# Attention with routed experts on one core: rows of the last ten expert tiles turned by the DMA, and a second staging buffer for weights

## The chip, the core and the metric

The kernel runs on one core of a Trainium2 chip. The metric is device time in microseconds (us) of one launch. Engines are named as in the profile: PE is TensorE (PEld its weight loads), DVE is VectorE, ACT is ScalarE, POOL is GpSimd, SP is SyncE, which issues most DMAs.

## The reference, cut to what matters

```python
q_rot, k_rot = (rotate(q), rotate(k))             # B=4, H=8, S=576, D=64
attn = softmax(scale * q_rot @ k_rot.T)
x = (attn @ v).transpose(0, 2, 1, 3).reshape(B, S, 512)
logits = x @ w_gate                               # 8 experts
for b in range(B):
    for s in range(S):
        fresh_e = int(np.argmax(logits[b, s]))
        e = fresh_e if s == 0 or local_gate[b, s] < 0.5 else prev_e
        prev_e = e
        h = np.maximum(x[b, s] @ w1[e], 0.0)      # 512 -> 1024
        out[b, s] = p[e] * (h @ w2[e])            # 1024 -> 512
```

A token keeps its predecessor's expert unless its gate falls below one half, so tokens have to be sorted by expert before the expert products.

## The kernel before, in words

The first part of the program is attention over pairs of heads, then routing. The second part, which the change touches, works through tiles of 128 tokens, each tile of one expert. There are 19 of them, numbered 0 to 18. Tiles 0 to 5 (KE = 6 of them) are filled from the first three batches; tiles 6 to 18, the late tiles, are sorted when the routing of the last batch is known. LAST is 18. Code for further tiles stands behind a condition and isn't entered with these inputs.

With the reference's inputs the experts get 1152, 0, 0, 500, 0, 0, 606 and 46 tokens. The early tiles take experts 0, 0, 0, 0, 3, 3; the late tiles take 0 five times (tiles 6 to 10), 3 twice (11, 12), 6 five times (13 to 17) and 7 once (18). A late tile loads and splits weights only where its expert differs from that of the tile before (`need`), which is so in tiles 6, 11, 13 and 18.

All products are in fp32 as three passes over operands split into a high and a low part (`PASSES`). A tile t goes through these steps:

- `gather(t)`: POOL fetches 128 rows of x, with the token's probability behind them, by an indirect DMA.
- `turn_x(t)`: PE turns the 128x512 rows in four transposes into `tx`, ACT writes the high part `xs` (L303), DVE the low part (L307).
- `first_product(t)`: 24 matmuls give `h`, 128x1024 (L933). The first half goes through ACT's Relu (L943) and is turned by PE in `turn_h` (`th`, L967). The second half is turned by the DMA: DVE copies it into two planes of 16-bit halves (L942), SP stores them to `inner` in DRAM (L944), `land_h` reads them back by a DMA transpose (`ht`, L951), and `split_landed` makes high and low parts (ACT L957, DVE L958).
- `second_product(t)`: 24 matmuls give `o` (L976); ACT scales it by the probability (`os`, L981), POOL scatters the rows by an indirect DMA (L982).

Weights of one expert are eight pieces of 128x1024 (512 KB): k = 0 to 3 are the first matrix, 4 to 7 the second. `load_pair(t, c)` loads pieces 2c and 2c+1 into the one staging buffer `stage`, inside a condition on `need`. `split_w(t, c)` makes high parts (POOL L877 or ACT L875) and low parts (DVE or POOL L878) in the same kind of condition, and then issues `load_pair(t + 1, c)`.

The order of all this is written by hand, for late tiles in the string `TILE`. A letter is a step that is recorded on every engine's queue at that point, and each engine then runs its own queue in order: f is a quarter of the first product of tile t, s a quarter of the second product of tile t-1 (a last s records `os` and the scatter), x `turn_x(t+1)`, A and B the splits of the first matrix for t+1, C and D those of the second matrix for t, h `turn_h(t)`, T `land_h(t)`, H `split_landed(t-1)`, g a gather.

## Time and profile before

| what | value |
|---|---|
| measured, median of 3 (lowest to highest) | 549.04 us (548.77 to 549.04) |
| profiled execution, its own time | 548.69 us |
| its span in the trace | 546.8 us |
| PE busy | 520.2 us, 95% of the span |
| DVE, ACT, POOL busy | 401.7, 334.1, 327.6 us |
| mean granted clock of PE | 0.994 of full speed |

Times in the views are microseconds from the start of the span. The late tiles run from 372.43, where the first product of tile 6 starts, to 537, where the last product ends. The profiled execution's own time is 1.9 us more than its span.

### The profile page before, as it was taken

To read this page: it belongs to the slowest core of one execution; us is meant where nothing else is said; L and a number is where in the kernel's file an instruction comes from. 1 tells how busy PE (TensorE), PEld (TensorE's weight loads), DVE (VectorE), ACT (ScalarE), POOL (GpSimd) and SP (SyncE) were. 2 spreads that over 40 slices of the span, in tenths; PEclk is the share of its full clock that TensorE was granted. 3 is DMA by queue.
4 is the path that set the end of the run, shared out by engine and by line. 5 is a ranking of instruction groups with operands and counts; after the bars stand their busy time and mean duration, and the time that the engine had idled before them with its cause. 6 is when DMAs were issued, how large, how long until landed. Compare 5 with 4: busy or idle time off the path is not lost. (4 is left out here: it accounts for less than half of the span.)

```text
span 546.8 us, 10672 instructions
## 1 busy us (share of the span) xinstructions
PE 520.2 (95%) x3280; PEld 459.5 (84%) x3281; DVE 401.7 (73%) x736; ACT 334.1 (61%) x754; POOL 327.6 (60%) x243
## 2 busy tenths in 40 slices
PE   7989999999999999998999999999999998999992
PEld 4788999999999999997888788887888886888871
DVE  6898999999999999999999845348422757522650
ACT  2899889888998999987667523351421333422340
POOL 2997989888777988986698202355412453411341
PEclk9999999999999999999999999999999999999997
DMA  8759688776887787885288214553437394635350
GB/s 249 297 123 230 180 242 236 175 200 184 229 229 180 210 223 203 214 220 146 34 201 233 70 27 167 166 220 120 171 98 241 107 352 138 200 102 183 117 184 25
DMA packets 62024, 97.35 MB, mean 178 GB/s; under 512 B 27969, under 2 KB 38209, under 8 KB 59010
## 3 DMA queue, kind: packets, MB, share of 16 engines
q1 hardware_dynamic: 58914, 86.84, 55.4%
q0 software_dynamic: 3040, 9.71, 5.7%
q8 instruction: 28, 0.46, 0.3%
q14 instruction: 42, 0.34, 0.2%
HBM read 76.98 MB, written 12.86 MB: 164 GB/s over the span
## 5 line engine op out<-in xcount | busy, mean ns | idle before, releaser
L976 PE MATMUL o<-w,hs 128*128 128x512 f32 x456 | 113.5, 398 | 2.2 <-DVE hs L307 1.0
L272 DVE TENSOR_REDUCE mn<-s 128x1 f32<-128x576 f32 x144 | 107.3, 746 | 3.6 <-PE s L267 2.2
L933 PE MATMUL h<-w,xs 128*128 128x512 f32 x444 | 106.1, 392 | 0.9 <-DVE xs L307 0.6
L289 ACT ACTIVATE e<-s,mn 128x576 f32<-128x576 f32 x128 | 95.2, 744 | 18.7 <-DVE mn L272 15.4
L267 PE MATMUL s<-m,qst 128*128 128x288 f32 x512 | 97.4, 310 | 5.4 <-ACT e L289 3.2
L307 DVE TENSOR_TENSOR ptl<-tm,pth 128x512 fp32r<-128x512 f32 x139 | 95.1, 684 | 6.5 <-ACT pth L303 4.1
L976 PEld LDWEIGHTS o<-w,hs 128*128 128x128 f32 x456 | 83.0, 188 | 19.8 <-DVE hs L958 1.4
L982 POOL DMA_INDIRECT out_dram<-os,sidx x19 | 23.5, 1238 | 126.8 <-ACT os L981 79.7
L933 PEld LDWEIGHTS h<-w,xs 128*128 128x128 f32 x444 | 82.6, 188 | 19.1 <-DVE w L878 1.1
L303 ACT CAST pth<-tm 128x512 fp32r<-128x512 f32 x139 | 80.8, 582 | 12.3 <-PE tm L325 11.2
L267 PEld LDWEIGHTS s<-m,qst 128*128 128x128 f32 x512 | 74.7, 188 | 12.2 <-ACT e L289 6.2
L325 PE MATMUL tm<-wid,e 128*128 128x128 f32 x512 | 77.0, 272 | 1.3 <-ACT e L289 0.5
L361 PE MATMUL pv<-pth,v 128*128 128x288 f32 x256 | 76.4, 314 | 0.4 <-DVE ptl L307 0.2
L361 PE MATMUL pv<-ptl,v 128*128 128x288 f32 x256 | 76.5, 314 | 0.0
L196 POOL TENSOR_TENSOR stage<-stage 128x1152 f32<-128x1152 f32 x26 | 69.0, 2665 | 10.5 <-DMA stage<-in_qk_dram 10.5
L878 DVE TENSOR_TENSOR w<-stage,w 128x1024 fp32r<-128x1024 f32 x41 | 56.8, 1424 | 22.3 <-POOL w L877 13.9
L325 PEld LDWEIGHTS tm<-wid,e 128*128 128x128 f32 x512 | 62.0, 140 | 2.2 <-DVE ptl L307 1.0
L361 PEld LDWEIGHTS pv<-pth,v 128*128 128x128 f32 x256 | 48.2, 188 | 2.8 <-DVE ptl L307 0.9
L361 PEld LDWEIGHTS pv<-ptl,v 128*128 128x128 f32 x256 | 48.3, 189 | 0.0
L943 ACT ACTIVATE hr<-h 128x512 f32<-128x512 f32 x12 | 7.2, 599 | 50.5 <-DVE hr L942 50.5
L307 DVE TENSOR_TENSOR hs<-th,hs 128x512 fp32r<-128x512 f32 x26 | 17.4, 687 | 27.3 <-ACTq L884 17.0
L197 POOL TENSOR_TENSOR stage<-stage 128x576 f32<-128x576 f32 x26 | 36.9, 1430 | 0.2
(195 smaller groups left out, 815.4 us busy)
## 6 DMA issues: line engine op xcount, KB each, us to landing
stage<-in_wts_dram SPq DMA_DIRECT2D x70, 512.0 KB
stage<-in_qk_dram SPq DMA_DIRECT2D x13, 1152.0 KB
stage<-in_wts_dram SPq DMA_DIRECT2D x9, 1024.0 KB
qst<-xq SPq DMA_DIRECT2D x56, 128.0 KB
stage<-in_v_dram SPq DMA_DIRECT2D x16, 320.0 KB
m<-xq SPq DMA_DIRECT2D x14, 288.0 KB
m<-xk SPq DMA_DIRECT2D x14, 288.0 KB
m<-xq SPq DMA_DIRECT2D x14, 256.0 KB
```

The lines of the kernel that those rows point to most:

```text
L196: engine.tensor_tensor(x, x, tab[:, 2 * f:2 * f + 2], op=ALU.mult)
L197: engine.tensor_tensor(rr[:, f], x[:, 0], x[:, 1], op=ALU.add)
L267: pe.matmul(st[:, h, lo:hi], lhs, keys[:, k0:k0 + hi - lo], start=(n == 0), stop=(n == len(parts_) - 1))
L272: dve.tensor_reduce(mn, s_t[g][:, :, 0:HALF], axis=AX.XY, op=ALU.min)
L289: act.activation(dst.rearrange("p (h s) -> p h s", h=2), s_t.pop(g)[:, :, 0:HALF], AF.Exp, bias=mn, scale=-1.0, accum_out=sums[:, col:col ...
L303: act.copy(hi, src)
L307: dve.tensor_tensor(lo, src, hi.bitcast(F32), op=ALU.subtract)
L325: pe.transpose(ps[:, k], src[:, k * P:(k + 1) * P], ident)
L361: pe.matmul(pv_t[p, u], lhs.rearrange("p c d -> p (c d)"), rhs, start=(n == 0), stop=(n == 9))
L878: (pool if k in on_pool else dve).tensor_tensor(lo, src, hi.bitcast(F32), op=ALU.subtract)
L933: pe.matmul(ps[:, c], xs_t[t][:, x, k], w[y][:, c * 512:(c + 1) * 512], start=(k == 0 and n == 0), stop=(k == 3 and n == 2))
L976: pe.matmul(ps, hs_t[t][:, x, k], w[y][:, (k % 2) * 512:(k % 2 + 1) * 512], start=(k == 0 and n == 0), stop=(k == 7 and n == 2))
```

## The change

Ten tiles, 9 to 18, get their x rows turned in the way that the second half of `h` already goes (`X_DMA` is 9). Letter P: POOL copies the gathered rows of tile t+3 into two planes of 16-bit halves (`planes_x`) and keeps the probability aside (`keep_prob`). Letter T: behind the transpose of `ht`, SP issues the transpose `xt` for tile t+2 and the store of the planes of t+3 to `turned`. Letter x: ACT and DVE split `xt` of tile t+1, which is now read from SBUF and no longer from PSUM. Gathers come two tiles earlier; tile 6 issues three.

The two pieces of the 16-bit planes of `h` are copied by ACT where DVE did it. H stands before A now, and D behind the last s.

The first matrix of tile t+3 is loaded behind D, at L, of tile t; even tiles use a second staging buffer `other`, in space that early tiles had used. Each load has 512 KB; pairs of 1024 KB are gone. The loads of the second matrix stay at C and D.

```diff
@@ -47,8 +47,9 @@
 SPREAD_LAST = 127
 
 TILE_EARLY = ("ffAffsfxBssgCsshD", "ffAffxfsBsCsgsshD", "fffAffxBssChsgssD", "ffAfffxBsssshsCDg", "ffAfffBsssxsshCgD", "fffxAffsBssgssChD")
-TILE = "ffAgffHfxBTssshsCDs"
-TILE_LAST = "ffxAffHfssBsChsDss"
+TILE = "ffHAgPfffxBTssshsCsDL"
+X_DMA = KE + 3
+TILE_LAST = "ffHfffsssChsDss"
 PULL = 3
 PE_LAG = 2
 
@@ -169,6 +170,7 @@
 
     qtail = [const.tile([P, 2, P], F32R, name="qtail")] * 2
     rows_d = dram.tile([NT + 1, DX], F32, name="rows_d")
+    turned_d = [dram.tile([P, 2, 512], U16, name=f"turned_{i}") for i in range(2)]
     inner_d = [dram.tile([P, 2, 512], U16, name=f"inner_{i}") for i in range(2)]
 
     qkl = stage[:, 0:2304].rearrange("p (f s) -> p f s", f=4)
@@ -804,6 +806,7 @@
         return [plan, codes] + slots(lambda: st["codes"], NBLK, KE, NLATE) + [first_gather, experts_of]
 
     NTILE = KE + NLATE
+    LAST = KE + U_LATE - 1
     w_t, x_t, xs_t, h_t, hs_t = {}, {}, {}, {}, {}
     w_done = set()
     regs = {}
@@ -815,8 +818,15 @@
         )
 
     w_stage = []
-
-    def staged(k):
+    other = []
+
+    def staged(k, t=0):
+        if k < 4 and KE < t <= LAST and t % 2 == 0:
+            if not other:
+                two = over.tile([P, 2304], F32, tag="xq", name="other_0")
+                other.extend(two[:, i * 1024:(i + 1) * 1024] for i in range(2))
+                other.extend(over.tile([P, 1024], F32, tag=f"qst{i}", name=f"other_{2 + i}") for i in range(2))
+            return other[k]
         return stage[:, k * 1024:(k + 1) * 1024] if k < 7 else w_stage[0][:, 0:1024]
 
     def load_w(t, k):
@@ -833,9 +843,8 @@
         if t in regs:
             e, need = regs[t]
             with tc.If(need > 0):
-                for k, n in ((6, 1), (7, 1)) if c == 3 else ((2 * c, 2),):
-                    to = stage[:, k * 1024:(k + n) * 1024] if k < 7 else staged(7)
-                    sp.dma_start(to, wts[bass.ds(e, 1), :, k * 1024:(k + n) * 1024])
+                for k in (2 * c, 2 * c + 1):
+                    sp.dma_start(staged(k, t), wts[bass.ds(e, 1), :, k * 1024:(k + 1) * 1024])
 
     def split_early(k):
 
@@ -849,7 +858,7 @@
         w_t[0, k] = hi, lo
         w_done.add((0, k))
 
-    need_t, w_own, landed = {}, {}, {}
+    need_t, w_own, landed, prob_of, xs_src, planes_of = {}, {}, {}, {}, {}, {}
 
     def needs_of(t):
 
@@ -870,7 +879,7 @@
         def parts():
             for d in range(2):
                 k = 2 * c + d
-                src, hi, lo = staged(k), w[:, d, 0], w[:, d, 1]
+                src, hi, lo = staged(k, t), w[:, d, 0], w[:, d, 1]
                 if k in on_act:
                     act.copy(hi, src)
                 else:
@@ -891,7 +900,7 @@
             w_done.add((t, k))
             if t <= KE:
                 load_w(t + 1, k)
-        if t > KE:
+        if t > KE and c > 1:
             load_pair(t + 1, c)
 
     def gather(t):
@@ -939,18 +948,40 @@
             act.activation(h, ps.rearrange("p c n -> p (c n)"), AF.Relu)
             return
         planes = h[:, 512:].bitcast(U16).rearrange("p (l n) -> p l n", l=2)
-        dve.tensor_copy(planes, ps[:, 1].bitcast(U16).rearrange("p (n l) -> p l n", l=2))
+        act.copy(planes, ps[:, 1].bitcast(U16).rearrange("p (n l) -> p l n", l=2))
         act.activation(h[:, 0:512], ps[:, 0], AF.Relu)
         sp.dma_start(inner_d[t % 2], planes)
 
     def by_dma(t):
         return KE <= t < LAST
 
+    def turn_by_dma(name, src):
+        x = pk_p.tile([P, S], F32, tag="pk", name=name)[:, 0:512]
+        sp.dma_start_transpose(x.bitcast(U16).rearrange("p (k n) -> p k n", k=4), src.rearrange("t l n -> (t l) n"))
+        return x.rearrange("p (k n) -> p k n", k=4)
+
     def land_h(t):
-        x = pk_p.tile([P, S], F32, tag="pk", name=f"ht_{t}")[:, 0:512]
-        sp.dma_start_transpose(
-            x.bitcast(U16).rearrange("p (k n) -> p k n", k=4), inner_d[t % 2].rearrange("t l n -> (t l) n"))
-        landed[t] = x.rearrange("p (k n) -> p k n", k=4)
+        landed[t] = turn_by_dma(f"ht_{t}", inner_d[t % 2])
+
+    def keep_prob(t):
+        p = lg_all.rearrange("p j e -> p (j e)")[:, 100 + t - KE:101 + t - KE]
+        pool.tensor_copy(p, x_t[t][:, DM:DM + 1])
+        prob_of[t] = p
+
+    def planes_x(t):
+        x = pk_p.tile([P, S], F32, tag="pk", name=f"xp_{t}")[:, 0:512]
+        planes = x.bitcast(U16).rearrange("p (l n) -> p l n", l=2)
+        pool.tensor_copy(planes, x_t[t][:, 0:DM].bitcast(U16).rearrange("p (n l) -> p l n", l=2))
+        keep_prob(t)
+        planes_of[t] = planes
+
+    def split_x(t):
+        xs = v2_p.tile([P, 10, 2, D], F32R, tag="v2", name=f"xs_{t}")
+        xs = xs.rearrange("p j c d -> p (j c d)")[:, 0:1024].rearrange("p (l k n) -> p l k n", l=2, k=4)
+        x = xs_src.pop(t)
+        act.copy(xs[:, 0], x)
+        dve.tensor_tensor(xs[:, 1], x, xs[:, 0].bitcast(F32), op=ALU.subtract)
+        xs_t[t] = xs
 
     def split_landed(t):
         x, hs = landed.pop(t), hs_t[t]
@@ -978,7 +1009,7 @@
             if k % 2 == 1:
                 yield k
         o = et_p.tile([P, S], F32, tag="et", name=f"os_{t}")
-        act.activation(o[:, 0:DM], ps, AF.Copy, scale=x_t[t][:, DM:DM + 1])
+        act.activation(o[:, 0:DM], ps, AF.Copy, scale=prob_of[t] if t in prob_of else x_t[t][:, DM:DM + 1])
         done = pool.indirect_dma_start(
             out=outf, out_offset=bass.IndirectOffsetOnAxis(ap=sidx[:, t:t + 1], axis=0),
             in_=o[:, 0:DM], in_offset=None, bounds_check=NT - 1, oob_is_err=False)
@@ -986,7 +1017,8 @@
         tc.declare_no_dep(done.ins, group="rows out", reason="rows of their own")
         tc.add_to_no_dep_group("rows out", done.ins)
 
-    LAST = KE + U_LATE - 1
+    def ahead(t):
+        return [u for u in ((KE + 2, KE + 3) if t == KE else (KE + 1,) if t == KE - 1 else (t + 3,)) if KE < u <= LAST]
 
     def experts_phase():
         for t in range(LAST + 1):
@@ -1000,15 +1032,20 @@
                             finish()
                         if t < LAST:
                             needs_of(t + 1)
-                        if KE < t + 2 <= LAST:
-                            expert_of(t + 2)
+                        for u in ahead(t):
+                            expert_of(u)
                     if k is not None:
                         yield t
                 elif c == "s":
                     if next(second, None) is not None:
                         yield t
                 elif c == "x" and t < LAST:
-                    turn_x(t + 1)
+                    if t + 1 >= X_DMA:
+                        split_x(t + 1)
+                    else:
+                        turn_x(t + 1)
+                        if t + 1 >= KE:
+                            keep_prob(t + 1)
                 elif c in "AB" and t < LAST:
                     split_w(t + 1, "AB".index(c))
                 elif c in "CD" and t > 0:
@@ -1016,16 +1053,31 @@
                 elif c == "h":
                     turn_h(t)
                     yield t + 1
+                elif c == "P" and t + 3 <= LAST:
+                    planes_x(t + 3)
                 elif c == "T":
                     land_h(t)
+                    if X_DMA <= t + 2 <= LAST:
+                        xs_src[t + 2] = turn_by_dma(f"xt_{t + 2}", turned_d[t % 2])
+                    if t + 3 <= LAST:
+                        sp.dma_start(turned_d[(t + 3) % 2], planes_of[t + 3])
+                elif c == "L":
+                    for u in ahead(t):
+                        for i in range(2):
+                            load_pair(u, i)
                 elif c == "H" and by_dma(t - 1):
                     split_landed(t - 1)
                 elif c == "g":
                     if t == 0:
                         gather(4)
                         gather(5)
-                    elif KE < t + 2 <= LAST:
-                        gather(t + 2)
+                    elif t == KE - 1:
+                        gather(KE + 1)
+                    elif t == KE:
+                        for u in range(KE + 2, KE + 5):
+                            gather(u)
+                    elif KE < t and t + 4 <= LAST:
+                        gather(t + 4)
         for _ in second_product(LAST):
             yield LAST
 
...
```

The order on the engines, at three places. First PE, in tile 14, from the end of its first product to the second product of tile 13 (`h_14`, `o_13`); before:

```order
L933 MATMUL h_14_7151<-w_1_5073,xs_14_7081 128x512 x11
L919 MATMUL tx_15_7224<-wid_93,x_15_7059 128x128 x4
L976 MATMUL o_13_7240<-w_2_5147,hs_13_7117 128x512 x9
L884 UNCONDITIONAL_BRANCH
L835 UNCONDITIONAL_BRANCH
L976 MATMUL o_13_7240<-w_2_5147,hs_13_7117 128x512 x3
L976 MATMUL o_13_7240<-w_3_5154,hs_13_7117 128x512 x6
L967 MATMUL th_14_0_7260<-wid_93,hr_14_7219 128x128 x4
```

and in the changed kernel:

```order
L942 MATMUL h_14_7248<-w_1_5075,xs_14_7175 128x512 x11
L1007 MATMUL o_13_7334<-w_2_5149,hs_13_7207 128x512 x10
L893 UNCONDITIONAL_BRANCH
L1007 MATMUL o_13_7334<-w_2_5149,hs_13_7207 128x512 x2
L1007 MATMUL o_13_7334<-w_3_5156,hs_13_7207 128x512 x6
L998 MATMUL th_14_0_7354<-wid_93,hr_14_7317 128x128 x4
```

The four transposes `tx` are gone; nothing else on PE moved.

Second SP, in tile 10, from the store of `h`'s planes (`inner_0<-hr_10`) and the landing of `ht_10` on; before:

```order
L944 DMA inner_0_104<-hr_10_6651 128x1024
L884 UNCONDITIONAL_BRANCH
L835 COMPARE_AND_BRANCH
L838 ISA
L838 DMA stage_94<-in_wts_dram 128x2048
L835 UNCONDITIONAL_BRANCH x2
L951 DMA_TRANSPOSE ht_10_6670<-inner_0_104 128x4x256
L884 UNCONDITIONAL_BRANCH
L835 COMPARE_AND_BRANCH
L838 ISA
L838 DMA stage_94<-in_wts_dram 128x2048
```

and in the changed kernel, from the same transpose on:

```order
L960 DMA_TRANSPOSE ht_10_6745<-inner_0_106 128x4x256
L960 DMA_TRANSPOSE xt_12_6747<-turned_0_104 128x4x256
L893 UNCONDITIONAL_BRANCH
L1063 DMA turned_1_105<-xp_13_6718 128x1024
L845 COMPARE_AND_BRANCH
L847 ISA
L847 DMA stage_94<-in_wts_dram 128x1024
L847 ISA
L847 DMA stage_94<-in_wts_dram 128x1024
L845 UNCONDITIONAL_BRANCH x2
```

Behind these stand three more conditional blocks of two loads each, and only then the store of `h`'s planes of tile 11; before, the first matrix's two loads stood on either side of that store.

Third DVE, in tile 12, around the split of the landed half (`hs_11<-ht_11`); before:

```order
L878 TENSOR_TENSOR w_0_5189<-stage_94,w_0_5189 128x1024 x2
L884 UNCONDITIONAL_BRANCH x2
L835 UNCONDITIONAL_BRANCH
L958 SCALAR_TENSOR_TENSOR hs_11_6833<-ht_11_6812,hs_11_6833 128x512
L942 COPY hr_12_6935<-h_12_6867 128x1024
L307 TENSOR_TENSOR xs_13_6939<-tx_13_6940,xs_13_6939 128x512
```

and in the changed kernel:

```order
L989 SCALAR_TENSOR_TENSOR hs_11_6915<-ht_11_6891,hs_11_6915 128x512
L893 COMPARE_AND_BRANCH
L887 TENSOR_TENSOR w_0_5191<-stage_94,w_0_5191 128x1024 x2
L893 UNCONDITIONAL_BRANCH x2
L983 TENSOR_TENSOR xs_13_7029<-xt_13_6893,xs_13_7029 128x512
```

The landed half is split ahead of the weights of tile 13, which now queue behind it, and the copy of the planes has left DVE.

## Rows read from the trace of the kernel before

**Rows 1.** Timeline of PE: the x transposes of tiles 8, 9, 17 and what follows.

```profile
402.52 0.60 PE L919 MATMUL tx<-wid,x 128*128 128x128 f32 x4
402.88 4.36 PE L976 MATMUL o<-w,hs 128*128 128x512 f32 x18
...
414.33 0.60 PE L919 MATMUL tx<-wid,x 128*128 128x128 f32 x4
...
511.63 0.60 PE L919 MATMUL tx<-wid,x 128*128 128x128 f32 x4
511.98 4.38 PE L976 MATMUL o<-w,hs 128*128 128x512 f32 x18
```

**Rows 2.** Timeline of PE in tile 12; brackets: idle before it, and releaser.

```profile
449.81 0.60 PE L919 MATMUL tx<-wid,x 128*128 128x128 f32 x4
...
453.36 0.73 PE L976 MATMUL o<-w,hs 128*128 128x512 f32 x2 [0.18 <-ACT hs L957]
455.10 1.20 PE L976 MATMUL o<-w,hs 128*128 128x512 f32 x4 [1.01 <-DVE hs L958]
456.86 0.66 PE L967 MATMUL th<-wid,hr 128*128 128x128 f32 x4 [0.56 <-ACT hr L943]
...
464.20 0.60 PE L919 MATMUL tx<-wid,x 128*128 128x128 f32 x4
```

**Rows 3.** Timeline of SP's DMA issues, tiles 10 to 12.

```profile
431.96 1.27 SPq L951 DMA_TRANSPOSE ht<-inner  x1
435.14 4.18 SPq L838 DMA_DIRECT2D stage<-in_wts_dram  x4
439.62 0.48 SPq L944 DMA_DIRECT2D inner<-hr  x1
...
448.61 1.27 SPq L951 DMA_TRANSPOSE ht<-inner  x1
```

**Rows 4.** Windows: us, busy us of each engine, PEclk, DMA share, GB/s.

```profile
489.35:491.42 2.07, 2.07 (x11) 1.70 (x10) 0.69 (x1) 1.07 (x2) 0.00 (x0) 1.00 0.34 127
491.42:494.95 3.53, 3.53 (x19) 2.93 (x18) 0.69 (x1) 1.04 (x2) 0.00 (x0) 1.00 0.36 74
437.00:448.00 11.00, 11.00 (x54) 9.07 (x54) 5.83 (x6) 5.09 (x7) 3.92 (x3) 1.00 1.00 390
432.50:444.30 11.80, 11.80 (x57) 9.80 (x56) 5.47 (x7) 3.49 (x6) 5.92 (x4) 1.00 0.84 288
```

**Rows 5.** Timeline in tile 12: ACT and DVE at the landed half.

```profile
452.67 0.63 ACT L957 ACTIVATE hs<-ht 128x512 fp32r<-128x512 f32 x1 [5.45 <-DMA ht<-inner]
...
453.47 1.57 DVE L958 SCALAR_TENSOR_TENSOR hs<-ht,hs 128x512 fp32r<-128x512 f32 x1
```

**Rows 6.** Timeline in tile 18, all engines.

```profile
518.03 5.62 PE L933 MATMUL h<-w,xs 128*128 128x512 f32 x24
...
520.56 1.94 SPq L838 DMA_DIRECT2D stage<-in_wts_dram  x3
...
526.20 1.05 POOL L877 TENSOR_SCALAR w<-stage 128x1024 fp32r<-128x1024 f32 x1 [5.56 <-DMA stage<-in_wts_dram]
...
527.62 3.20 DVE L878 TENSOR_TENSOR w<-stage,w 128x1024 fp32r<-128x1024 f32 x1 [5.42 <-ACT w L875]
...
528.37 2.08 PE L976 MATMUL o<-w,hs 128*128 128x512 f32 x8
...
530.74 1.27 DVE L307 TENSOR_TENSOR hs<-th,hs 128x512 fp32r<-128x512 f32 x2
...
531.47 5.28 PE L976 MATMUL o<-w,hs 128*128 128x512 f32 x22 [1.01 <-DVE hs L307]
```

**Rows 7.** Groups by line and shape, 372 to 537 us: busy, mean ns, idle before.

```profile
L877 POOL TENSOR_SCALAR w<-stage 128x1024 fp32r<-128x1024 f32 x14 | 16.2, 1167 | 19.4 <-DMA stage<-in_wts_dram 13.6 <-PE o L976 4.2 <-PE h L933 1.5
L942 DVE COPY hr<-h 128x1024 uint16<-128x1024 uint16 x12 | 14.7, 1221 | 15.8 <-PE h L933 14.9 <-DVEq L884 0.8
L878 POOL TENSOR_TENSOR w<-stage,w 128x1024 fp32r<-128x1024 f32 x4 | 9.6, 2398 | 0.3
L939 ACT ACTIVATE hr<-h 128x1024 f32<-128x1024 f32 x1 | 1.0, 1029 | 2.2 <-PE h L933 2.2
```

**Rows 8.** Timeline of POOL in tile 6.

```profile
376.64 1.57 POOL L908 DMA_INDIRECT x<-rows_d,gidx  x1 [0.67 <-POOLq L884]
382.35 1.05 POOL L877 TENSOR_SCALAR w<-stage 128x1024 fp32r<-128x1024 f32 x1 [4.14 <-DMA stage<-in_wts_dram]
383.48 2.40 POOL L878 TENSOR_TENSOR w<-stage,w 128x1024 fp32r<-128x1024 f32 x1
```

More of the change, by code (lines that the diff above doesn't have):

```diff
@@ L1038, in rest @@
                 expert_of(t)
+                regs[t] = regs[t][0], None
                 for k in range(8):
```

## The prediction

> **What bounds the kernel now.** I read the timeline of PE first, tile by tile, to see where PE stands still; then, at each such place, the timelines of the other engines and of SP's issues; then windows, for the load of the DMA engines.
>
> In most late tiles nothing but PE counts. The x transposes of tiles 8 and 9 start 11.81 us apart (402.52 and 414.33) [rows 1], and in a window of one tile PE is busy all of 11.80 us, at a granted clock of 1.00, while DVE, ACT and POOL are busy 3.5 to 5.9 us [rows 4]. So a matmul that goes away shortens such a tile by its own length, and a step added to another engine costs nothing until it makes PE wait.
>
> PE does wait in two places behind tile 7. Tile 12: from its x transposes to those of tile 13 it is 464.20 - 449.81 = 14.39 us, 2.58 more than 11.81. The brackets beside the matmuls name 1.75 of that as idle; the rest hides in modelled ends, so I go by starts [rows 2]. The waits name the landed half `ht` of tile 11. On SP four loads (1024, 512, 512 and 1024 KB by the code) went out from 435.14 on, the store of `h`'s planes at 439.62, and the transpose that needs this store only at 448.61 [rows 3]: the store lay behind 3 MB. ACT could take the landed half at 452.67 [rows 5], and PE wanted it at 449.81 + 0.36 + 12 x 0.24 = 453.1 [rows 1, 2].
>
> Tile 18: 8 matmuls take 531.47 - 528.37 = 3.10 us where 22 take 5.28, that is 0.24 each; 8 should take 1.92, so 1.18 us are lost. What is late is DVE's low part of `hs` (530.74), queued behind a weight split of 3.20 us that began at 527.62; and that waited for weights issued at 520.56, which POOL could touch at 526.20 [rows 6].
>
> **The change, part by part.**
>
> *The x transposes leave PE in ten tiles.* They stand ahead of the second products in tiles 8 to 17 (letter x makes tile t+1 = 9 to 18). One costs the time from its start to that of the next matmul: 402.88 - 402.52 = 0.36 in tile 8, 511.98 - 511.63 = 0.35 in tile 17 [rows 1]. Ten make **3.55 us**. Nothing comes back on PE.
>
> *What takes their place.* Per tile: a copy to planes on POOL, a store of 256 KB, a DMA transpose of 256 KB, and splits by ACT and DVE that existed before with another source. The trace has no POOL copy of 16-bit pieces. The nearest POOL rows, also 1024 elements a partition, are 1.17 us with one input and 2.40 with two [rows 7]; a copy has one input, so I take 1.2 and keep 2.4. It has room: POOL is busy 5.92 of 11.80 us in a tile with weights to split [rows 4]. The store keeps the 16 DMA engines busy 0.34 x 2.07 = 0.70 us and the transpose 0.36 x 3.53 = 1.27 us, read from windows that hold one of them each [rows 4]. SP pays 1.27 us for the transpose and up to 0.48 for the store [rows 3]. `xt` has a whole tile of slack, because tile t fetches it for t+2. Priced at nothing where the DMA queue is short; where it isn't, see the next part.
>
> The Trainium skill ("Advanced Engine Details and Errata", X-Bar Transpose) says that on this chip a transposing DMA is as fast as a regular one; here 1.27 us stand against 0.70 for the same bytes, so the trace disagrees. By the rule the two new transfers would add about 1.4 us of DMA time to a tile, by the rows 1.97.
>
> *Planes of `h` on ACT.* DVE needs 1.22 us for this copy; ACT's nearest row, 1024 elements from the same tile of PSUM, is 1.03 [rows 7]. The Relu waited for the copy before and does so now, so the chain gets no longer. Worth nothing where PE doesn't wait; it takes the copy out of DVE's queue behind weight splits.
>
> *Loads and the order of SP.* This touches tile 12. Of weights, the same 4 MB go out for tiles 11 and 13 together; now all eight loads stand ahead of the store of tile 11, where the last 1 MB stood behind it. Against this, they start earlier. The transpose of `ht_10` began at 431.96 [rows 3]; three tiles are by then 0.36 shorter, and the planes no longer queue on DVE, which I estimate at up to 2 us; then come two transposes and a store (2.9 us). So the loads begin between 431.8 and 433.8; I take 432.8. With 4.2 MB of weights, 0.26 of the store, and 0.52 of a gather and a scatter, 5.0 MB run ahead of the landing. At the 390 GB/s of the full queue [rows 4] that is 12.8 us, and with 1.4 for what a store takes beyond its own transfer (2.07 - 0.70) it has landed at 447.0. From the transpose's issue to ACT's start it was 452.67 - 448.61 = 4.06, and 453.36 - 452.67 = 0.69 more to the matmul [rows 2, 3, 5]. That gives 451.75. PE, five transposes shorter, asks at 453.1 - 1.8 = 451.3. So under 0.5 us of 2.58 stays. On DVE the splits of tile 13's first matrix and of `xs` now queue behind that landed half; they are done just as PE asks for them. I leave 0.5 us for both together: **2.1 us** gained. The bounds: with the early start nothing is left of the stall (2.58); with the late start and the rate of the whole stretch before (435.14 to 448.61 for 3.9 MB, 0.29 MB/us [rows 3]) the landed half is ready at 455.8, a stall of 4.6, which is 2.0 more than before.
>
> *Halves in the last tile.* POOL can begin on the first 512 KB when half as much has landed, 1.3 us sooner at 390 GB/s. Its two steps (1.05 and 2.40) then end at 528.4, DVE's split, which runs long beside POOL, ends near 529.6 and the first low part near 530.3, just when PE's third pass asks for it (528.37 + 8 x 0.24). The loads are also issued sooner, since DVE is rid of the planes that made the steps before them late in tile 17. So the stall goes: **1.1 us**, bounds 0 and 1.18.
>
> The row that DVE's split took 3.20 us beside POOL's 2.40 bears on the new work too: `xs`'s low part had one operand in PSUM and now has both in SBUF. The Trainium skill ("SBUF — State Buffer", Who interferes with whom) says that a DVE instruction with two inputs from SBUF and a POOL instruction that reads SBUF shut each other out for a whole instruction, and the trace agrees here. By that rule each tile's new POOL copy may hold DVE up by its 1.2 to 2.4 us; the sum would stay as it is, since DVE has over 6 us free in a tile with weights to split (5.47 busy of 11.80) [rows 4].
>
> *Tile 6.* POOL issues three gathers (1.57 us for one) and then waits for the second to land before it can copy planes, all ahead of its weight split that ran from 382.35 to 385.88 [rows 8]. Some 3 us later it is still done ahead of the second product of tile 7, which starts one tile (11.81) before 402.88 [rows 1], at 391.1. Priced at 0, at most 1 us lost if that copy costs 2.4.
>
> **The sum.** 3.55 + 2.1 + 1.1 = 6.75. The profiled execution's 548.69 becomes 541.9; it stands 0.35 under the median of the runs, so the forecast for the median is **542.3**.
>
> **The rivals.** 0.2% is 1.1 us, and about what a measurement of this kernel can tell from no change.
>
> 1. *The queue keeps the stall in tile 12* or makes it longer. For it: the DMA engines are busy 0.84 of 11.80 us in tile 11 before [rows 4], 9.9 us, and 1.97 more is 11.9 in a tile of 11.46, so the queue can't empty there. Against it: the transposes of that tile stand behind the store that counts. Gain 3.55 + 1.1 = 4.65, less up to 2.0: 544.4 to 546.4. Chance 0.20.
> 2. *POOL's copy is slow*, and POOL sets the length of ten tiles. Without weights POOL issues a scatter and a gather in a tile, 1.0 to 1.6 us each; so it falls behind from a copy of some 9.5 us on, four times its dearest row of this size (2.40) [rows 7]. At 11 us the tiles would last about 13, and ten of them 1.2 us more than before each: 561. For it: no row shows such a copy, and 16-bit pieces two apart are not what these rows move. Chance 0.06, the other sign.
> 3. *The freed PE time goes elsewhere*: tiles stay 11.81 long, because `xs` or `ht` arrive with that period, and the stalls stay. Against it: every engine but PE has half a tile free. 548 to 549.6, chance 0.05.
>
> **How the numbers follow.** My forecast, gain 5 to 7.3, has 0.69: 541.7 to 544. The range takes in rival 1: 541.5 to 546.5, and leaves out rivals 2 and 3 and the far ends of the others, together about 0.2. Faster by over 0.2%: 0.69 plus most of rival 1, 0.87. Within: 0.05. Slower: rival 2 and what a longer queue than my bound could do, 0.08.
>
> **What would show it.** Right: in tiles 8 to 17 the second product starts straight behind the first, and starts lie 11.46 apart; in tile 12 under 1 us is lost; in tile 18 DVE's low parts come ahead of PE. POOL's copy takes 1 to 2.4 us. Wrong: tiles that stay at 11.8, PE waiting for `xs` (then the new DMA path is late), PE waiting for `hs` at tile 12 by over 2.6 (the burst), or a stall at the start of tile 7's second product (tile 6's gathers).

## Result, and the profile after

The changed kernel takes **554.4 us** (median of 6 runs, 552.86 to 555.4), the kernel before, beside it, 548.9 (6 runs, 547.76 to 551.7): ratio 1.0094, interval 1.0066 to 1.0122. It is slower; I had forecast 542.3. The profiled execution took 555.18 us with a span of 553.4 and a mean granted clock of 0.983.

PE's timeline of the changed kernel, in order: the second product in tile 7 (from 393.24), tile 8 (from 400.13), tile 9's first line (411.50), the second products in tiles 10 and 12, each with the first line of the tile behind it, and the end of tile 18. A bracket is PE's idle time and who ended it.

```profile
393.24 0.48 PE L1007 MATMUL o<-w,hs 128*128 128x512 f32 x1
394.31 4.16 PE L1007 MATMUL o<-w,hs 128*128 128x512 f32 x17 [0.59 <-POOLq L893]
...
400.13 5.62 PE L942 MATMUL h<-w,xs 128*128 128x512 f32 x24
405.59 4.25 PE L1007 MATMUL o<-w,hs 128*128 128x512 f32 x18
...
411.50 5.62 PE L942 MATMUL h<-w,xs 128*128 128x512 f32 x24
...
428.98 2.88 PE L1007 MATMUL o<-w,hs 128*128 128x512 f32 x12
433.68 2.16 PE L1007 MATMUL o<-w,hs 128*128 128x512 f32 x6 [1.82 <-ACT hs L988]
...
438.85 5.64 PE L942 MATMUL h<-w,xs 128*128 128x512 f32 x24
...
450.23 5.61 PE L942 MATMUL h<-w,xs 128*128 128x512 f32 x24
455.68 2.88 PE L1007 MATMUL o<-w,hs 128*128 128x512 f32 x12
463.16 2.93 PE L1007 MATMUL o<-w,hs 128*128 128x512 f32 x6 [4.60 <-ACT hs L988]
465.89 1.05 PE L998 MATMUL th<-wid,hr 128*128 128x128 f32 x4
...
469.30 5.63 PE L942 MATMUL h<-w,xs 128*128 128x512 f32 x24
...
537.01 7.34 PE L1007 MATMUL o<-w,hs 128*128 128x512 f32 x30
```

Tile 8 shows the change at work: no x transposes stand between the products, and the tile lasts 411.50 - 400.13 = 11.37 us, where it was 11.81 [rows 1]. Tile 18 is cured: 30 matmuls without a break, where 1.18 us were lost [rows 6]. But tile 12 lasts 469.30 - 450.23 = 19.07 us, 7.70 over an undisturbed one; before it lost 2.58 [rows 2]. Tile 10, where nothing was lost before, takes 15.3, and tile 7 loses 0.9.

Windows of PE around the two long pauses; the columns are as in [rows 4]: busy time and count of PE, PEld, DVE, ACT and POOL, then PE's granted clock, DMA share and GB/s.

```profile
431.86:433.68 1.82, 0.00 (x1) 0.00 (x1) 0.02 (x1) 0.68 (x2) 0.00 (x0) 1.00 1.17 240
433.68:438.85 5.17, 5.17 (x17) 3.88 (x18) 5.17 (x6) 3.39 (x5) 0.00 (x0) 0.67 0.23 86
...
458.56:463.16 4.60, 0.00 (x0) 0.00 (x0) 0.02 (x1) 0.68 (x2) 1.23 (x3) 0.93 0.96 205
463.16:469.30 6.14, 6.14 (x16) 4.84 (x17) 6.14 (x7) 3.39 (x5) 0.00 (x0) 0.50 0.41 75
469.30:474.77 5.47, 5.47 (x25) 4.52 (x24) 1.02 (x2) 1.32 (x2) 3.31 (x4) 1.00 0.84 207
```

Behind the pauses the granted clock was 0.67 and 0.50. Of PE's two levels, 2.4 and 1.2 GHz, that is the lower one for all of the second stretch and for part of the first. The same work (12 matmuls and four transposes) takes 3.03 us undisturbed (tile 11 has its second product from 444.32 to 450.23, 5.91 us, less 2.88 for its first twelve matmuls); here it took 5.17 and 6.14. So tile 10 lost 1.82 by waiting and 2.14 by the clock, tile 12 lost 4.60 and 3.11.

What came late was again the landed half. SP's issues in tiles 8 to 11:

```profile
410.38 0.34 SPq L953 DMA_DIRECT2D inner<-hr  x1
412.46 1.26 SPq L960 DMA_TRANSPOSE ht<-inner  x1
413.81 1.30 SPq L960 DMA_TRANSPOSE xt<-turned  x1
...
416.73 5.91 SPq L847 DMA_DIRECT2D stage<-in_wts_dram  x4
424.18 0.35 SPq L953 DMA_DIRECT2D inner<-hr  x1
428.43 1.79 SPq L960 DMA_TRANSPOSE ht<-inner  x1
...
438.14 1.26 SPq L960 DMA_TRANSPOSE ht<-inner  x1
...
442.04 5.78 SPq L847 DMA_DIRECT2D stage<-in_wts_dram  x8
449.31 0.35 SPq L953 DMA_DIRECT2D inner<-hr  x1
458.06 1.27 SPq L960 DMA_TRANSPOSE ht<-inner  x1
```

ACT takes the landed half (L988) and then copies the planes of the next one (L951). Its timeline:

```profile
419.27 0.63 ACT L988 ACTIVATE hs<-ht 128x512 fp32r<-128x512 f32 x1 [6.83 <-DMA ht<-inner]
419.80 1.00 ACT L951 COPY hr<-h 128x1024 uint16<-128x1024 uint16 x1
...
433.00 0.63 ACT L988 ACTIVATE hs<-ht 128x512 fp32r<-128x512 f32 x1 [8.53 <-DMA ht<-inner]
...
462.48 0.63 ACT L988 ACTIVATE hs<-ht 128x512 fp32r<-128x512 f32 x1 [9.43 <-SPq L845]
```

*Tile 12* is as in the forecast's first rival: the eight loads go out from 442.04, the store at 449.31 lies behind them, and `ht_11` is issued only at 458.06. *Tile 10* is a chain over two tiles. `ht_8`, issued at 412.46, reaches ACT at 419.27, after 6.81 us; in the kernel before such a transpose took 3.2 to 4.1, apart from the two named at the end of this document, and `ht_10` here took 441.97 - 438.14 = 3.83. Behind it in ACT's queue wait the planes of tile 9 (419.80). They are done at 420.80, but their store comes only at 424.18, behind four loads that take SP 5.91 us, because two of them waited for the landings of `ht_8` and `xt_10` (us in total, times, longest):

```profile
SPq L847 <- DMA ht<-inner: 2.0, 1, 2.0
...
SPq L847 <- DMA xt<-turned: 1.2, 1, 1.2
```

So `ht_9` reaches ACT at 433.00, 1.14 after PE had asked (431.86).

POOL shows what ran beside `ht_8`, and why tile 7 lost 0.9. Its timeline:

```profile
387.19 1.03 POOL L974 COPY xp<-x 128x1024 uint16<-128x1024 uint16 x1 [4.21 <-DMA x<-rows_d,gidx]
...
389.91 1.04 POOL L886 TENSOR_SCALAR w<-stage 128x1024 fp32r<-128x1024 f32 x1 [0.44 <-POOLq L893]
391.04 3.22 POOL L887 TENSOR_TENSOR w<-stage,w 128x1024 fp32r<-128x1024 f32 x1
...
412.72 1.02 POOL L1013 DMA_INDIRECT out_dram<-os,sidx  x1 [7.79 <-ACTq L893]
414.06 1.03 POOL L917 DMA_INDIRECT x<-rows_d,gidx  x1 [0.31 <-issue]
```

A scatter went out at 412.72, 0.26 us behind `ht_8`, and a gather at 414.06, 1.60 behind it. In tile 6 POOL waits 4.21 us for a gather and copies planes only then; its weight split, at 382.35 before [rows 8], comes at 389.91 and ends just when PE goes on at 394.31.

One more part of the difference is probably not the change's: this execution enters tile 6 at 374.62, where before it was 372.43. In its first 20 us the clock once fell to 0.69 of full speed; in the profiles of the twelve kernels below tile 6 starts between 371.95 and 373.66.

### The profile page after: what moved, and what is told of

Same layout as the page of the kernel before. It is cut to its first block, busy times and chain, and to the rows that moved or that the text cites. A ratio compares the mean times of both kernels' runs of the same rounds, so it can differ in the third digit from the quotient of the medians.

```text
span 553.4 us, 10665 instructions
## 1 busy us (share of the span) xinstructions
PE 523.2 (95%) x3241; PEld 459.8 (83%) x3241; DVE 386.3 (70%) x724; ACT 345.2 (62%) x766; POOL 340.5 (62%) x266
## 5 line engine op out<-in xcount | busy, mean ns | idle before, releaser
L1007 PE MATMUL o<-w,hs 128*128 128x512 f32 x456 | 117.8, 407 | 7.1 <-ACT hs L988 6.4
L1007 PEld LDWEIGHTS o<-w,hs 128*128 128x128 f32 x456 | 85.7, 193 | 27.8 <-ACT hs L988 8.2
L291 ACT ACTIVATE e<-s,mn 128x576 f32<-128x576 f32 x128 | 95.2, 744 | 19.7 <-DVE mn L274 16.3
L887 DVE TENSOR_TENSOR w<-stage,w 128x1024 fp32r<-128x1024 f32 x37 | 52.4, 1449 | 15.4 <-ACT w L884 9.3
L989 DVE SCALAR_TENSOR_TENSOR hs<-ht,hs 128x512 fp32r<-128x512 f32 x12 | 9.1, 757 | 60.7 <-ACT hs L988 60.0
L988 ACT ACTIVATE hs<-ht 128x512 fp32r<-128x512 f32 x12 | 7.6, 632 | 57.0 <-DMA ht<-inner 35.7
```

Source lines behind the costliest of these rows:

```text
L291: act.activation(dst.rearrange("p (h s) -> p h s", h=2), s_t.pop(g)[:, :, 0:HALF], AF.Exp, bias=mn, scale=-1.0, accum_out=sums[:, col:col ...
L887: (pool if k in on_pool else dve).tensor_tensor(lo, src, hi.bitcast(F32), op=ALU.subtract)
L1007: pe.matmul(ps, hs_t[t][:, x, k], w[y][:, (k % 2) * 512:(k % 2 + 1) * 512], start=(k == 0 and n == 0), stop=(k == 7 and n == 2))
```

## The experiments

Each was timed in five rounds beside the kernel before. "Lost" is the time of a tile beyond an undisturbed one of the same kernel (11.35 to 11.37 us, or 11.82 where PE turns x; 11.82 for tile 7), from the starts on PE in the profiled execution. That is one execution of each kernel, and its own time can lie off the median: 547.56 against 552.12 in experiment 1, 541.25 against 543.31 in 7, 544.19 against 542.53 in 10.

| kernel | median, us | ratio to before, interval | lost in tile 7 | 8 to 10 | 11, 13 | 12 | 14 to 17 |
|---|---|---|---|---|---|---|---|
| before | 548.9 | | 0 | 0 | 0 | 2.59 | 0.2 |
| changed | 554.4 | 1.0094 (1.0066-1.0122) | 0.9 | 4.6 | 0 | 7.70 | 0.5 |
| 1 loads back | 552.12 | 1.0031 (0.9998-1.0063) | 0.9 | 2.9 | 0 | 2.56 | 1.3 |
| 2 no DMA path of x | 546.37 | 0.9939 (0.9919-0.996) | 0.5 | 0.1 | 0 | 0.57 | 0 |
| 3 loads a tile later | 556.99 | 1.0144 (1.0106-1.0183) | 0.9 | 1.3 | 10.8 | 1.04 | 1.3 |
| 4 pauses filled | 552.64 | 1.0074 (1.0048-1.0101) | 2.4 | 1.6 | 0 | 6.23 | 1.7 |
| 5 xt first | 547.46 | 0.9975 (0.9954-0.9997) | 1.0 | 0 | 0 | 6.78 | 0.1 |
| 6 no gathers | 548.52 | 1.0000 (0.9983-1.0016) | 0.8 | 0 | 0 | 6.76 | 0.9 |
| 7 loads back, xt first | 543.31 | 0.9927 (0.9894-0.9961) | 1.3 | 0 | 0 | 1.08 | 0 |
| 8 stores alone | 547.60 | 0.9981 (0.9961-1.0001) | 0.9 | 0 | 0 | 1.21 | 0.2 |
| 9 = 7, planes behind split | 542.02 | 0.9867 (0.9845-0.989) | 0.2 | 0.1 | 0 | 1.10 | 0 |
| 10 = 9, pair behind landing | 542.53 | 0.9859 (0.9839-0.988) | 0.3 | 0 | 0 | 0.01 | 2.0 |
| 11 = 5, one xt less | 545.96 | 0.9943 (0.9924-0.9962) | 1.3 | 0 | 0 | 3.79 | 0.5 |
| 12 neither part | 545.55 | 0.9937 (0.9917-0.9957) | 0.2 | 0 | 0 | 0.01 | 0 |

**1. Loads back.**

```diff
-        if t > KE and c > 1:
+        if t > KE:
             load_pair(t + 1, c)
```

with `staged` and `expert_of` as before and nothing at L.

> The changed kernel, with the first matrix of the next expert loaded again where it was before the change (behind its split, into the one staging buffer); the x rows stay with the DMA. Theory Q (the weight loads that now stand ahead of a store of h's planes make the landed half late, in tiles 10 and 12): tile 10 loses nothing, tile 12 at most the 2.6 us of before, and PE's clock stays up; ten tiles are 0.44 shorter. 544 to 547 us. Theory T (the new transposes and stores of x are what makes the landed half late, wherever the loads stand): tiles 10 and 12 still lose 3 us or more each, 551 us or more.

Measured: the median is where theory T has it, the tiles lie between the two. Tile 12 is back at 2.56, 5.1 us less than in the changed kernel; but tile 8 loses 2.1, tile 10 0.7 and tile 14 1.2. The runs scatter from 546.41 to 552.85, and the profiled one is the second shortest.

**2. No DMA path of x.**

```diff
-X_DMA = KE + 3
+X_DMA = KE + 99
-                elif c == "P" and t + 3 <= LAST:
+                elif c == "P" and X_DMA <= t + 3 <= LAST:
-                    if t + 3 <= LAST:
+                    if X_DMA <= t + 3 <= LAST:
                         sp.dma_start(turned_d[(t + 3) % 2], planes_of[t + 3])
```

> The changed kernel without the DMA path of x: all x rows are turned on PE again, and no planes of x are copied, stored or fetched. The second staging buffer and the early loads stay. Theory Q: eight loads in a row still stand ahead of the store of tile 11, so tile 12 still loses 4 us or more, clock included; 550 to 554 us. Theory T: no transposes of x, no late half: tiles 10 and 12 lose at most what they lost before; 546 to 549 us.

```profile
434.33 6.03 SPq L847 DMA_DIRECT2D stage<-in_wts_dram  x8
...
454.09 0.63 ACT L988 ACTIVATE hs<-ht 128x512 fp32r<-128x512 f32 x1 [5.29 <-SPq L845]
```

Theory Q falls as I had put it: with the same eight loads in a row tile 12 loses 0.57. From the first of them to ACT's `hs` it is 19.8 us (434.33 to 454.09) and in the changed kernel 20.4 (442.04 to 462.48). What differs is when PE asks, counted from the first load: 20.4 us later here (454.7), 16.5 in the changed kernel (458.56).

**3. Loads a tile later**, in `ahead`:

```diff
-        return [u for u in ((KE + 2, KE + 3) if t == KE else (KE + 1,) if t == KE - 1 else (t + 3,)) if KE < u <= LAST]
+        return [t + 2] if KE < t + 2 <= LAST else []
```

> The changed kernel with the early loads issued one tile later (those of tile t+2 at L of tile t, where it was t+3), so that never more than four loads stand in a row, and in another tile than the four of the second matrix. Theory Q: no store of planes waits behind 2 to 4 MB of loads any more; tiles 10 and 12 lose under 1 us each; 542 to 546 us. Theory T: the transposes of x are unchanged, so the losses stay; 551 us or more.

Slower than either theory had it: PE now waits in the first product, for the matrix itself and for `xs`, which DVE has queued behind its split. That loses 5.9 us in tile 11 and 4.8 in tile 13, clock included. This tells nothing of Q or T; that the loads can't come this late is all it shows.

**4. Pauses filled.**

```diff
+FILL = {10: 7, 12: 18}
...
+            n_s = 0
...
+                    n_s += 1
+                    if n_s == 2 and t in FILL:
+                        fill = ps_s.tile([P, 2, 512], F32, tag="s", name=f"fill_{t}")
+                        for _ in range(FILL[t]):
+                            pe.matmul(fill[:, 0], hs_t[t - 1][:, 0, 0], w_t[t - 1, 4][0][:, 0:512], start=True, stop=True)
```

> The changed kernel with matmuls that compute nothing needed put where PE pauses: 7 in tile 10 and 18 in tile 12, behind the twelfth matmul of the second product (0.24 us each: 1.7 and 4.3 us). If the pause is what lowers PE's clock behind it, the pauses stay as long (1.8 and 4.6) but the 2.1 and 3.1 us of half clock behind them go: 549 to 550 us, granted clock 1.00 in both tiles. If the clock falls for another reason, 554 us as before, with the same slow matmuls behind.

Its windows in tile 12: the fill, what is left of the pause, and what follows. (Tile 10 tests nothing here: ACT began on the landed half at 429.94, before PE asked at 430.39.)

```profile
454.67:458.91 4.24, 4.24 (x19) 3.19 (x17) 0.00 (x0) 0.00 (x0) 2.96 (x4) 1.00 0.69 152
458.91:460.48 1.57, 0.01 (x2) 0.00 (x1) 0.02 (x1) 0.68 (x2) 0.00 (x0) 1.00 1.24 169
460.48:464.09 3.61, 3.61 (x17) 2.68 (x18) 3.61 (x5) 3.29 (x5) 0.00 (x0) 1.00 0.23 87
```

PE waited even longer in tile 12 (5.8 us with the fill), yet the clock stayed at 1.00 and the work behind took 3.61 where it took 6.14: it was PE's idleness that lowered the clock there. The mean granted clocks agree: 0.983 to 0.988 in the six runs of the changed kernel, 0.990 to 0.996 in the six of this one. The time missed the forecast by 3 us: this execution lost 1.5 us more than the changed kernel in tile 7 and 1.2 more in tiles 14 to 17, and by medians alone the fill shows no gain (the intervals overlap).

**5. xt first.**

```diff
-                    land_h(t)
                     if X_DMA <= t + 2 <= LAST:
                         xs_src[t + 2] = turn_by_dma(f"xt_{t + 2}", turned_d[t % 2])
+                    land_h(t)
```

> The changed kernel with two lines swapped: at T the transpose of x (xt, tile t+2) is issued ahead of the transpose of the landed half (ht, tile t), in the 2 us in which SP waits for the store of h's planes anyway. Loads stay where the change put them. Theory A (ht's data counts as landed only when the xt transpose queued right behind it has run too, and that one is stretched where a gather runs beside it): tiles 9, 10 and 17 lose nothing, tile 12 under 1 us, clock up; 542 to 545 us. Theory B (it is the added transfers as such, their bytes and their issue on SP, in whatever order): losses stay, 551 us or more.

Two lines bring 7 us by the medians. Tiles 8 to 11 and 13 to 17 run undisturbed, 11.34 to 11.37 each; tile 12 still loses 6.78, which theory A had not expected.

**6. No gathers.**

```diff
                     elif KE < t and t + 4 <= LAST:
-                        gather(t + 4)
+                        x_t[t + 4] = x_t[KE + 4]
```

> The changed kernel without the gathers of tiles 11 to 18, which take the rows of tile 10 instead (their output is of other rows); everything else is as in the changed kernel. Theory A with its second half (the gather stretches the transposes from 1.3 to some 4 us): tiles 9 and 10 no longer lose, tile 12 at most 2.5 us; 544 to 548 us. If gathers have no part in it: tiles 9, 10 and 12 lose as in the changed kernel, 553 to 555 us.

The gathers left out are those of tiles 11 to 18. The time is just over the range of theory A. Tiles 8 to 10 lose nothing either, with xt still behind ht. That does not single out the gather, because the scatters moved with it: they start 0.46 and 2.21 us behind `ht_7` and `ht_8` here, 0.08 and 0.26 in the changed kernel. And experiment 4, the changed kernel's own program up to tile 10, speaks against the gather alone. There `ht_8` has a transpose `xt` behind it and a scatter and a gather beside it, and is in use after 3.14 us:

```profile
411.23 1.26 SPq L961 DMA_TRANSPOSE ht<-inner  x1
...
412.10 1.02 POOL L1014 DMA_INDIRECT out_dram<-os,sidx  x1 [7.76 <-ACTq L894]
413.45 1.04 POOL L918 DMA_INDIRECT x<-rows_d,gidx  x1 [0.32 <-issue]
...
414.37 0.63 ACT L989 ACTIVATE hs<-ht 128x512 fp32r<-128x512 f32 x1 [2.55 <-DMA ht<-inner]
```

The traces point to the scatter's moment. In the changed kernel and experiments 1, 3, 4 and 6 there are 50 landed halves with an `xt` behind them. Eight had a scatter start within 0.3 us of their issue, and seven of these took 5.4 to 8.0 us (the other 3.38); of the other 42 only two took over 5. No experiment moved the scatter by itself, so this stays a reading. Tiles 14 to 17 still lose 0.9 in all, and tile 12 is unmoved (6.76).

**7. Loads back and xt first.**

> The kernel with the loads back where they were before the change, with the same swap: xt ahead of ht. Theory A: tile 8 and tile 14, which lost 2.1 and 0.7 us with the loads back, lose nothing, tile 12 at most the 2.6 us of before; 544 to 546 us, and the runs lie close together. Theory B: 550 to 553 us, as without the swap. Against the kernel with the swap alone it shows what the early loads are worth: 2 to 3 us by my forecast.

Faster than both kernels and than my forecast, though the runs don't lie close together: two of eight took 548.2 and 548.4. The early loads, which I had credited with 2.1 us, cost 4 (547.46 against 543.31); the intervals just overlap, but tile 12 loses 6.78 with them and 1.08 without.

**8. Stores alone.**

```diff
-                    if X_DMA <= t + 2 <= LAST:
-                        xs_src[t + 2] = turn_by_dma(f"xt_{t + 2}", turned_d[t % 2])
-                    if t + 1 >= X_DMA:
+                    if False:
                         split_x(t + 1)
```

> The changed kernel with the planes of x copied by POOL and stored by SP as in the change, but never fetched: no xt transposes, x turned on PE in all tiles (nothing uses what was stored). Theory A (the xt transposes do it): as without the whole DMA path of x, 546 to 547 us, no loss in tiles 9, 10 and 17. Theory B (POOL's copies, the stores, or SP's waits for them): losses in tiles 10 and 12 as in the changed kernel, 554 us or more.

As theory A has it in tiles 8 to 10, which lose nothing; tile 12 loses 1.21 even with eight loads in a row. POOL's copies and the stores aren't free, though: against experiment 2 the ratio is 0.9981 and not 0.9939, with 0.4 us more lost in tile 7 and 0.6 more in tile 12.

**11. One xt less**: experiment 5 without `xt_13`, whose place is between the store of tile 11 and `ht_11`.

```diff
-                    if X_DMA <= t + 2 <= LAST:
+                    if X_DMA <= t + 2 <= LAST and t + 2 != 13:
-                    if t + 1 >= X_DMA:
+                    if t + 1 >= X_DMA and t + 1 != 13:
```

> The changed kernel with xt ahead of ht (early loads as in the change, eight in a row ahead of the store of tile 11), and one single transpose of x left out: the rows of tile 13 are turned on PE. It would have been issued between the store of tile 11 and ht_11. If the burst of loads alone is what makes tile 12 lose 6.8 us, it still loses 5 us or more: 546 to 548 us. If it is the burst and the transpose of x that runs between the loads and ht, beside a gather and a scatter, tile 12 loses 2 us or less: 542 to 544 us.

In between: tile 12 loses 3.79 (0.4 of it by the x transposes back on PE) and 6.78 with `xt_13`. The pause is 2.74 us and not 5.07, and behind it the clock stays up:

```profile
453.48:456.22 2.74, 0.00 (x1) 0.00 (x1) 0.02 (x1) 0.69 (x2) 0.76 (x1) 1.00 0.65 200
456.22:459.82 3.60, 3.60 (x16) 2.68 (x17) 3.60 (x5) 3.25 (x5) 0.00 (x0) 1.00 0.34 100
```

In experiment 5 the same stretch, with its clock:

```profile
451.56:456.63 5.07, 0.00 (x0) 0.00 (x1) 0.02 (x1) 0.68 (x2) 1.25 (x3) 0.97 1.00 222
456.63:461.90 5.27, 5.27 (x19) 4.21 (x20) 5.27 (x6) 3.68 (x6) 0.00 (x0) 0.71 0.54 120
```

Not all of this is `xt_13`. ACT starts on the half 2.06 us after PE asked, and 4.39 in experiment 5. Of the difference, 0.98 is the landing (19.84 us behind the first load, 20.82 in 5), 0.49 is PE, which turns `x` itself and asks later, and 0.86 is that the loads went out 2.38 us behind the tile's start and not 3.24, which the edit doesn't touch.

The last figure is the one to follow. In all seven kernels with eight loads in a row ACT takes the half 18.2 to 20.8 us behind the first load. Without transposes of `x` (experiments 2 and 8) that load goes out 0.21 and 1.13 us behind tile 11's start, and ACT has the half before PE asks. With them (changed, 4, 5, 6 and 11) it goes out 2.4 to 5.5 behind, and ACT starts 2.1 to 5.1 us after PE asked.

**12. Neither part**: experiments 1 and 2 together.

> The changed kernel with neither the DMA path of x nor the early loads: x is turned on PE in all tiles and the loads stand where they were before; what is left of the change is the planes of h on ACT, the order of H and D, loads in halves, and the early gathers. It completes a table of two by two: both parts 554.4, x on the DMA alone 552.1, early loads alone 546.4. If the stall in tile 18 goes because of the early loads, it is still there here and the time is 548 to 549 us; if it goes because of the halves and the copy taken from DVE, tile 18 is 1.0 shorter, tile 12 loses up to 2.6 as before, and the time is 547 to 548 us.

Better than expected. Tile 18 is cured here too (17.67 us against 18.72), so the early loads aren't needed for it; and tile 12 loses nothing, which no theory of mine had:

```profile
445.62 5.61 PE L942 MATMUL h<-w,xs 128*128 128x512 f32 x24
...
451.42 4.36 PE L1007 MATMUL o<-w,hs 128*128 128x512 f32 x18
...
457.44 4.93 PE L942 MATMUL h<-w,xs 128*128 128x512 f32 x21
```

SP sends the loads of this stretch from 432.99, 0.8 us ahead of tile 11's start (433.8); before it was 435.14, 2.6 behind it, after a wait of 1.4 us for DVE's queue (0.6 here).

**9. and 10. Toward a better kernel.** Experiment 9 is 7 with an order of its own for tile 6:

```diff
+TILE_FIRST = "ffHAgfffxBssshsCPTsDL"
```

> The kernel with the loads back and xt ahead of ht, and in tile 6 POOL copies the planes of x behind its weight split and no longer ahead of it (T moves behind it too). There POOL waited 4.6 us for a gather that lay behind ten weight loads, its split came at 387.7 and PE paused at the second product of tile 7. If that wait is the cause, the split is back at some 382, tile 7 lasts 11.8 us where it lasted 13.1, and the time is 1 to 1.5 us under the 543.3 of the kernel without this edit: 541.5 to 543. If the copy only changes places with something else that PE needs: 543 to 545 us.

POOL's timeline in tile 6: the split is back at 383.68, the copy follows.

```profile
383.68 1.04 POOL L887 TENSOR_SCALAR w<-stage 128x1024 fp32r<-128x1024 f32 x1 [1.44 <-DMA stage<-in_wts_dram]
384.81 2.41 POOL L888 TENSOR_TENSOR w<-stage,w 128x1024 fp32r<-128x1024 f32 x1
387.15 2.05 POOL L975 COPY xp<-x 128x1024 uint16<-128x1024 uint16 x1
```

Tile 7 loses 0.2 where it lost 1.3. At 0.9867 this is 1.3% faster than before. Experiment 12, with x on PE in all tiles, has 0.9937, so here the DMA path of x gains some 0.7%. Experiment 10 adds to it:

```diff
-        if t > KE:
+        if t > KE and c != 1:
             load_pair(t + 1, c)
...
                 elif c == "L":
-                    pass
+                    if t + 2 <= LAST:
+                        load_pair(t + 2, 1)
```

> The kernel of the run above, and the second 1 MB of the next expert's first matrix is issued behind the landing of ht and not ahead of it, so that nothing but x's transpose lies between the store of h's planes and ht. Theory Q (each MB of loads ahead of the landed half costs up to 2.6 us of it at 390 GB/s): the 1.1 us still lost in tile 12 fall under 0.5: 540.5 to 542.5 us. If the 1 MB behind the store had time to run while SP waits for the store anyway, no change: within 0.5 us of the run above. If it comes too late for the first product of tile 13: slower by 2 us or more.

Tile 12 loses nothing any more, but in the profiled execution tile 14 lost 2.0, and the time is the same: inconclusive.

## Why the prediction was wrong

*The x transposes (3.55): right, and small.* An undisturbed tile became 0.44 shorter, not 0.36: the 18 matmuls behind the transposes also go from 4.36 or 4.38 to 4.25. POOL's copy took 1.03 to 1.12 (1.2 taken), ACT's planes 1.00; the second rival is out.

*Tile 18 (1.1): size right, cause wrong in part.* It is 1.05 shorter with and without the early loads.

*Tile 12 (2.1 gained): the step that failed.* The lateness of `ht_11` was worked out as 0.45 us and came to 4.60; with the clock behind it the tile lost 7.70 where the forecast left 0.5, more than half of what the forecast missed. By its steps: the loads began 3.19 us behind tile 11's start and not 1.4, since the two microseconds that I gave the planes for leaving DVE did not come (`ht_10` went out 0.71 us ahead of the tile's start, 0.55 before) and two transposes, a store and what stands between took 3.9 us of SP and not 2.9; from the first load to `ht_11` 16.0 us passed, not 14.2; from there to ACT 4.42, not 4.06. PE asked about when I had said it would, 19.7 us behind tile 11's start. 4.6 is also the upper bound that I gave this wait (its working gives 4.5), and rival 1 named the place. In experiments 2 and 8, without the new transposes, the loads began 0.21 and 1.13 us behind the tile's start.

*What no bound held: the clock.* I priced a wait at its length. Behind those of 1.82 and 4.60 us PE lost another 2.14 and 3.11. Experiment 4 shows for tile 12 that the idleness is its cause; the price is read from traces, because by the medians the fill gained 1.8 us with overlapping intervals.

*"`xt` has a whole tile of slack ... priced at nothing": wrong.* The slack of `xt` was right; what it delays is `ht`. Queued behind `ht`, it made tiles 8 to 10 lose 4.6 us in the profiled execution and tile 17 0.5. Experiment 5 shows it, where the swap alone takes both away; experiments 2 and 8, without `xt`, lose at most 0.1 there. The Trainium skill ("DMA: Bandwidth & Descriptors", Issuing engines are not separate DMA queues) says that DMAs of SP and GpSimd run on the same 16 engines and interleave; the 6.81 us of `ht_8` beside POOL's scatter and gather fit that, and the 3.14 in experiment 4 show that it isn't all. What has to come with the `xt` behind, a gather or a scatter at the moment of issue, stays open, and so does why a landed half waits for the transpose behind it: I have shown what takes the loss away, not the mechanism inside the queue.

*Tile 6 (0, at most 1 lost): 0.9*, near the bound. Not the copy was slow: it waited 4.21 us for a gather.

*The early loads with the second staging buffer* brought nothing with either state of x: 0.9939 against 0.9937 without the DMA path, 1.0094 against 1.0031 with it, 0.9975 against 0.9927 with xt first. What had made tile 12 late before was cured by the small edits: planes on ACT, the order of H and D, loads in halves, early gathers. Experiment 12 holds them all at once, so which of them it is stays open.

## What to carry to other kernels

Before a transfer is called hidden, look what stands behind and beside it in the queue of the transfer that PE waits for: here two swapped lines and the loads' old place turned 554.4 us into 543.3. Price a wait of PE with the clock that it costs: here waits of 6.42 us cost another 5.25. And take a change of many parts apart in a table of two by two: the gain came from its small edits (experiment 12) and from x on the DMA (9 against 12), the loss from how the parts met on SP's queue.

## What was not expected of the hardware

The clock doesn't fall behind each pause. It stayed at 1.00 behind 1.58 and 2.01 us (experiment 1, tiles 8 and 12) and 2.74 (experiment 11), and fell behind 1.82 in the changed kernel (0.67), 4.60 (0.50), 4.71 (0.65, experiment 6) and 5.07 (0.71, experiment 5). So length alone does not decide it.

A transposing DMA of 256 KB took 3.2 to 4.1 us from issue to use in the kernel before, and 5.4 to 8.0 in seven of the eight cases where a second transpose was queued behind it and a scatter started within 0.3 us of its issue (`ht_7`: 5.65 in the changed kernel, 7.98 in experiment 1). In six cases with such a scatter and no transpose behind (experiments 2, 5, 8 and 12) it took 3.1 to 4.1. A weight load issued some 0.65 us ahead of it goes with the same: 5.41 and 6.78 for `ht_9` and `ht_16` before.
